# 64-key attention blocks in two-tile and eight-tile shapes, V projected by tokens, in a two-layer transformer kernel

## The chip, the cores and the metric

The kernel runs on one core of a Trainium2 chip. The metric is device time in microseconds (us) from one launch; lower is better. The engines of the core run side by side and each works through its own list in order: TensorE (PE; PEld is its weight load), VectorE (DVE), ScalarE (ACT), GpSimd (POOL) and SyncE (SP), which issues nearly all DMAs.

## The reference

Twice over, a residual attention and a residual token mixer, on S = 2048 tokens of D = 512 features in bf16 (F = 1792; shortened here):

```
def _A_ref(x, wqkv, wo):
    H = 32; Dh = D // H; W = 256
    qkv = (x @ wqkv).reshape(B, S, 3, H, Dh)
    scores = jnp.einsum("bhqd,bhkd->bhqk", q, k) * (Dh ** -0.5)
    mask = (idx[:, None] - idx[None, :] >= 0) & (idx[:, None] - idx[None, :] < W)
    p = _softmax(jnp.where(mask, scores, -1e9), axis=-1)
    return jnp.einsum("bhqk,bhkd->bqhd", p, v).reshape(B, S, D) @ wo
def _B_ref(x, w1, b1, w2, b2):
    u = _gelu(jnp.einsum("bsd,sf->bdf", _layernorm(x), w1) + b1)
    return (jnp.einsum("bdf,fs->bds", u, w2) + b2).transpose(0, 2, 1)
x = x + _A_ref(_layernorm(x), A_wqkv, A_wo)
x = x + _B_ref(_layernorm(x), B_w1, B_b1, B_w2, B_b2)
x = x + _A_ref(_layernorm(x), A_wqkv, A_wo)
x = x + _B_ref(_layernorm(x), B_w1, B_b1, B_w2, B_b2)
```

## The kernel before

Everything stays in on-chip memory between the stages. Weights and x come by DMA on SyncE's queue; only the result goes back.

**Attention.** A layer is cut into four quarters Q of 512 queries and, in each, four groups t of eight heads. A 128-row block of q or k holds the eight heads of a group, 16 rows each. For a group the keys come in blocks of 32, in nine steps m (`NB = 9`: 256 keys of window and one block); in step m each 32-query block i meets the key block kb = i - (i - m) % 9, so that one step fills 512 query columns with up to three runs of columns (`bank_segments`). The scores use the array as four tiles of 64x64 (line 797): r picks the upper or lower 64 rows, c the even or odd heads; k_sb holds each 32-key block twice, with one head of a pair zeroed in each copy, and q_sb holds q twice, even and odd 32-row strips.

```
for r in range(2):
    rows = slice(64 * r, 64 * r + 64)
    for c in range(2):
        last = e.matmul(ps[64 * c:64 * c + 64, 2 * half + r, 32 * i0:32 * i1],
                        lhsT=k_sb[rows, ring, t, kb % 16, :], rhs=q_sb[rows, t, c, 32 * i0:32 * i1],
                        start=True, stop=True, skip_group_check=True, tile_position=(64 * r, 64 * c))
```

The result of a step fills two PSUM banks (0 and 1, or 2 and 3). ScalarE takes the exponential of both into one of six slots of p_sb (line 808, `NSLOT = 6`). VectorE or GpSimd multiplies the 64 columns at the two edges of the window by a triangle (line 825). Then the V product adds the step into banks 4 and 5, again as four 64x64 tiles (line 846); v_all holds V per 32 keys and two heads, with a column of ones for the sum of the softmax. After the ninth step two copies (line 442) take the banks to oU and o2; after each second group, DMAs collect the denominators (den_c) and merge o2 into oU. A quarter later line 871 inverts the denominators, line 889 spreads the inverses over the rows by a matmul, and line 896 multiplies, giving oT, which the output projection (line 762) turns into an addition to x (line 766).

**Side jobs.** Between the steps, TensorE does the work of the next groups: transposes of the normalised x (lines 569 and 582), the projections of K and Q (line 593: four matmuls of the full 128x128 array, 512 columns each), and of V (line 697, also the full array, weights stationary, so that V comes out with its features on the rows). V is then turned by a 32x32 transpose on VectorE (line 700) and spread with zeros into v_all (line 712, VectorE, GpSimd or ScalarE). Line 634 masks K on its way to k_sb; four small DMAs carry q's strips from qt to q_sb. They all use banks 6 and 7.

**The mixer.** The first product (line 987) runs the full array over 16 token tiles for each of 14 blocks of F, then gelu (line 994). For ten of the 14 blocks the lower eight token tiles are done ahead, during the attention, by `paired` (line 609), which works in 64x64 tiles; line 992 adds that part. The second product (line 1033, full array) goes tile by tile into x; in the first layer, its last eight tiles run through `paired` during the second layer's attention.

**The order.** Each engine's list is written out by hand: tables in the file (`LINES`, `ORDER`, `BANKS`), packed as text, say which operation stands where, and the waits between engines follow from what each operation reads and writes. TensorE's matmuls are marked "full" (the 128x128 array) or "cells" (64x64 tiles).

Of the kernel before, what the change touches and what calls it, by code (L numbers as in the profile page):

```python
# [23 lines left out]


# [4 lines left out]
def _table(*text):  # L30
# [5 lines left out]
    'c-pO%NfLlC2n6Z*|D!$VA(pZwQ02iO5IRgWGvj$=s}a1_t)7LW%>DZDUfy1PqA2I%kl8c?b5B|cGg6XlcP%#(x1TjeVa`gOe{yPcK<L$?wAm@}'  # L36
    'VkysiU77XM`Cn79HbaE`*=AYKIH|352Ds;6D^<qc%}i^DBpz)O@D)yLnj()z{$97jIlPxA?E)0O0EP')
ORDER = _table(
    'c-jTQ17HvU00h8C*0OEeT()i7ww7(%wr$(CZSxKgh_DC-BLspY6ao+$$q^f25FX(W5)ly<5fB5B5g(Bd577||DG(D$5C;hn7YPsz8ITC6kqn8E'
    '6xp#48IclckPoSl4QY`HMUW1eksDc%9t{u$Igu4PPyl6+7rBrJg^?eDD2O^JijpXV;;4dRD31~-h0<t`%BYC4D2FDfh6<>ON~nr%sE*pGfm*1C'  # L40
    'uIPhCXo~unfVyaohG>jd7>O2WgJx)nb{K?CXpOe$fR5;lE|`lR=!Ny@hwd1Np6H8F7=XbThHVH!e+<QNOha#sz!)6D5RAuYjKeI9#bivyOiaWi'
    'Ou=-_!3@mCJj};gEW`pV#R)9OA}ql&ti&p;zz3|w2JFTfY{EKh#8xcE4s5}8?7~hw#%0{a9_+_Ktj1m(z-HXT5gf)boWe((!BL#YN!-9C9LH&#'
    '!$n*Lc?B164cGAlw{R1;aR+hu0Qd0-uka90@dPjM9Ix>b&+rzB_y+Is4quR*pYR=@@eO|vnqL9_#xI!v@E2kThGZIsWf(?aAWJYZgE2fKF)G6`'
    'fH7Esu^5HX8J9m1it!nfu^EpE8Jr22go&Ay$(WJRn35@&nyHwU*_e(Q7?GKoo|%}HjhKZwn4P(pn|V2ytyq)!nUjT>hxu5LMOc)DS%Ae^ip5xl'
    'l~|r7S(T+(ku_L_)mWC5S&Ow<opo8C^;m}u*?>*ioNd^WP1u3W*qWW$j&0eVo!F5**o{5ei(T1;ec7A+*^gs6h{M>J137|2IGm$6n%y~plNiLI'
    'oXU|L&xstv>72r8oW<E3$C;eRxm>{cT*yUS#-&`z6<ovRoWnlc#?{=-bzIMD+`!3P!d+a<jl9gOyuwx7#GAa%&Ai1M+`{eL!L8iMJ>1Lv+{cqV'
    '!Bf1z(>%^&yvU<G$0Iz$!#u!)Jj+8o&-=W@+q}a^e9Gs1$9sIhXMD&f{K&g}%ny9cmwdw)e8snX&)@vaPyE7f45LW;&Y%2B3;Mx7{L7U3MJc!v'
    '=pRFh3awxYp->8^hzhF+3a`wHtf-2q=n7C2MN@1QR9wYUd^J)WB~c=kR&~WwLZwk+C07d7Rc@tMDrHn!^-)%3S4(A3E@e?R<y2nfQGVr90Zmp1'
    '1*)*Rsf-G#go>+_%Bj36sfvOWL)BDKHC0(vRYSE@TlLjYO_Wac)LadeT8-6AEtE;EltanXRPEG8om5h-)m3d(K^@gaWz|!iRZRU<RK3+h1Jz4|'
    ')mOtbK!Y??b<|!XHA15_R!cQn<FsEhH9_MwMUym7(==7nHACGsOS3gs{k2eYG+&FgM9XwktF%%pv|KwiTx+yi>oi6iwN@LnS?je;o3vFsG*R2N'  # L50
    'OIx%@yR}ybbWlfhSjTlpr*uN6bxy~0QfG8t7j;3G^iEH;NY`~)w{=6ebWL}3RrmBn4|P`dO+D8GJ<=Op(FfhvK0Vemeb!sO)_eWXC;ie_z0`O8'
    '(@%ZTU(tVbS1<HR!3@hG9MT^Z%Ap<H-}GDI9N;((ba+R0SVwaNM{-0*bxg;0DJODVM{#_|a6;#B7{_uF$8!QFcVZ`VN~dyCr*L$qab;(87N>So'
    'cXd{0a4u(dI%ju!_jev=b0ODuPUm(}7jy|1aWQ9d8K-qg=XC{_c6nEHK38%z7jR+Ma9P)NRTp;^S9cvZa6>nC6PI&KH+O5davQgEdv|ax_iz{2'
    'bA5MmH#c%m_jNP(a$65}9}jepTX=*Ad6<WKxJP@G$9s%BySFF0pT~KEC%L<)d9tT_fM<E8XLzpXc)pkWh>v-J7kagidaB2Ih}ZbAr+ATPdx=l@'
    'lo$J?k9&oedYM;xmDhT`*Lj0?dY5;5kN0|;cX+G!d!sk`kT-j~xA=hf`Jm7EhR^$wullra`i^h;uJ8G*&-sEc`nF&Aim&;)pZl`!`;i~}i68ix'
    'pZcL+`KA8@K7;B`')
# [255 lines left out]
NB = 9  # L312
# [851 lines left out]
```

## Time and profile before

| | |
|---|---|
| median of 3 runs | 496.06 us (495.64 to 497.09) |
| span of the profiled execution | 495.9 us (the page gives no other time for it) |
| TensorE matmuls | 472.4 us busy, 95% |
| VectorE | 325.5 us, 66% |
| ScalarE | 320.6 us, 65% |
| GpSimd | 211.4 us, 43% |
| granted TensorE clock | 1.00 |

Busy times are averages over stages with different limits. The attentions lie between the first and last exponential of each layer, 15.7 to 162.8 us and 235.8 to 399.6 us. A matmul's duration contains the latency of the pipeline, so several can overlap; the time from one start to the next says more. The first matmul after a change of tile shape is sometimes missing from the records.

### The profile page before, as it was taken

What the parts mean: (1) busy time and instruction counts of PE and PEld (TensorE: products, weight loads), DVE (VectorE), ACT (ScalarE), POOL (GpSimd) and SP (SyncE); (2) the same over time, 40 slices, a digit from 0 to 9 for tenths busy, and PEclk for the clock granted to TensorE, in tenths of its full rate; (3) what the DMA queues carried; (4) which work ended last, traced back from release to release, by engine and by line L of the source; (5) the groups of instructions that cost most, each with busy time, mean ns of one, the idle gap of its engine ahead of it and who ended that gap; (6) DMA issues with size and microseconds to landing.
All of it is one profiled execution on the core that took longest, in us unless ns stands there. A gap on an engine that the chain in (4) does not pass through costs nothing.

```text
span 495.9 us, 19594 instructions
## 1 busy us (share of the span) xinstructions
PE 472.4 (95%) x8478; PEld 272.3 (55%) x8550; DVE 325.5 (66%) x661; ACT 320.6 (65%) x392; POOL 211.4 (43%) x372
## 2 busy tenths in 40 slices
PE   8899999999989999999999998998999999999997
PEld 3455566554767444445555875666557654444444
DVE  7999888977763763357895467976996557331222
ACT  3899999998989403502977779889899941340000
POOL 5889546564664310002676445467475411100000
PEclk9999999999999999999999999999999999999999
DMA  6732212131413631331101321024233464040651
GB/s 211 76 99 82 73 55 82 62 99 43 122 56 114 196 106 58 91 98 52 33 18 42 112 79 48 5 75 140 80 91 109 136 189 130 10 138 33 203 169 63
DMA packets 78597, 45.58 MB, mean 92 GB/s; under 512 B 9008, under 2 KB 77488, under 8 KB 78512
## 3 DMA queue, kind: packets, MB, share of 16 engines
q1 hardware_dynamic: 74640, 44.32, 30.4%
q0 software_dynamic: 3872, 0.02, 1.3%
q8 instruction: 67, 1.10, 0.9%
q14 instruction: 18, 0.15, 0.1%
HBM read 33.56 MB, written 2.10 MB: 72 GB/s over the span
## 4 chain that ended last, share of the span: by engine, by line
PE 78%; DVE 9%; ACT 5%; issue 4%; DMA 2%; SPq 2%; POOL 1%; DVEq 0%; ACTq 0%; POOLq 0%
PE ps L1033 14%; PE ps L987 13%; PE ps L609 12%; PE ps L797 10%; PE ps L846 9%; PE ps L593 7%; PE ps L762 5%; ACT p_sb L808 4%; PE ps L697 4%; PE ps L521 2%; SPq L436 2%; PE ps L889 1%; DMA oU<-o 1%; DVE p_sb L825 1%; DVE vt L700 1%
## 5 line engine op out<-in xcount | busy, mean ns | idle before, releaser
L808 ACT ACTIVATE p_sb<-ps 128x1024 bf16<-128x1024 f32 (+8 forms) x288 | 261.4, 975 | 28.7 <-PE ps L797 24.8
L825 POOL TENSOR_TENSOR p_sb<-p_sb,edge 128x256 bf16<-128x256 bf16 (+2 forms) x266 | 131.2, 499 | 111.7 <-ACT p_sb L808 97.8
L797 PE MATMUL ps<-q_sb,k_sb 64*64 64x288 bf16 (+8 forms) x2816 | 107.9, 249 | 4.5 <-ACT p_sb L808 4.3
L846 PE MATMUL ps<-p_sb,v_all 64*34 64x288 bf16 (+17 forms) x2816 | 89.1, 245 | 1.8 <-DVE p_sb L825 0.8
L797 PEld LDWEIGHTS ps<-q_sb,k_sb 64*64 64x64 bf16 x2816 | 59.1, 106 | 51.4 <-ACT p_sb L808 23.7
L846 PEld LDWEIGHTS ps<-p_sb,v_all 64*34 64x34 bf16 (+1 forms) x2816 | 60.6, 100 | 12.1 <-issue 3.6
L593 PE MATMUL ps<-xhT,wqkv 128*128 128x512 bf16 x212 | 55.3, 380 | 4.1 <-issue 3.0
L539 POOL TENSOR_TENSOR rstd<-vare,mhalf 128x4 f32<-128x4 f32 (+1 forms) x17 | 16.6, 976 | 81.0 <-DVE vare L537 57.3
L825 DVE TENSOR_TENSOR p_sb<-p_sb,edge 128x128 bf16<-128x128 bf16 (+2 forms) x134 | 35.5, 279 | 20.3 <-ACT p_sb L808 18.0
L1037 DVE SCALAR_TENSOR_TENSOR x_sb<-ps,b2col,x_sb 128x512 bf16<-128x512 f32 x23 | 17.0, 748 | 43.3 <-PE ps L1033 42.7
L527 DVE BATCH_NORM_STATS2 stats<-x_sb 128x6 f32<-128x512 bf16 x64 | 42.7, 681 | 0.6
L609 PE MATMUL ps<-xh_sb,w1low 64*64 64x512 bf16 x640 | 41.7, 377 | 0.1
L634 DVE TENSOR_TENSOR k_sb<-ps,half 128x1024 bf16<-128x1024 f32 (+1 forms) x31 | 36.5, 1176 | 5.5 <-PE ps L593 5.0
L549 ACT ACTIVATE xh_sb<-x_sb,shift,rstd 128x512 bf16<-128x512 bf16 x12 | 9.5, 812 | 45.2 <-POOL shift L543 29.4
L1033 PE MATMUL ps<-ubuf,w1buf 128*128 128x512 bf16 x165 | 37.2, 379 | 0.2
L712 POOL TENSOR_TENSOR v_all<-vt,even 128x1024 bf16<-128x1024 f32 (+2 forms) x22 | 33.0, 1504 | 5.0 <-DVE vt L700 2.7
L1033 PE MATMUL ps<-ubuf,oU 128*128 128x512 bf16 x149 | 34.3, 379 | 0.3
L994 ACT ACTIVATE ubuf<-ps,b1col 128x512 bf16<-128x512 f32 x28 | 18.5, 686 | 23.9 <-DVE ps L992 20.0
L697 PE MATMUL ps<-xhT,wqkv 128*128 128x512 bf16 x112 | 30.0, 380 | 3.7 <-issue 1.3
L593 PEld LDWEIGHTS ps<-xhT,wqkv 128*128 128x128 bf16 x240 | 19.4, 98 | 24.8 <-issue 4.2
L992 DVE TENSOR_TENSOR ps<-ps,ubuf 128x512 f32<-128x512 f32 x20 | 14.0, 699 | 26.5 <-PE ps L987 26.4
L762 PE MATMUL ps<-wo_sb,oT 128*128 128x512 bf16 x117 | 29.4, 380 | 1.7 <-issue 0.8
(93 smaller groups left out, 545.5 us busy)
## 6 DMA issues: line engine op xcount, KB each, us to landing
w1buf<-in_B_w_dram SPq DMA_DIRECT2D x30, 256.0 KB
w1buf<-in_B_w_dram SPq DMA_DIRECT2D x42, 128.0 KB
w1low<-in_B_w_dram SPq DMA_DIRECT2D x40, 128.0 KB
oU<-in_B_w_dram SPq DMA_DIRECT2D x18, 256.0 KB
oU<-o SPq DMA_DIRECT2D x16, 256.0 KB
q_sb<-qt SPq DMA_DIRECT2D x120, 32.0 KB
xhT<-in_B_w_dram SPq DMA_DIRECT2D x4, 512.0 KB
k_sb<-in_B_w_dram SPq DMA_DIRECT2D x4, 512.0 KB
```

Source lines behind the costliest of these rows:

```text
L527: dve(lambda e: e.bn_stats(stats[:, t, :], x_sb[:, t, :]), 690, prio, reads=[R("x", t)], writes=[R("stats", t)])
L593: last = e.matmul(ps[:, b, :], lhsT=wqkv[:, c, c0:c0 + P], rhs=xhT[:, buf, c, :], start=(c == 0), stop=(c == 3))
L609: last = e.matmul(ps[64 * h:64 * h + 64, banks[r ^ swap], :], lhsT=lhs(r ^ swap, c, rows, 64 * h), rhs=rhs(r ^ swap, c, rows), start=(c == ...
L634: return e.tensor_tensor(dst, src.unsqueeze(2).to_broadcast([P, n, 2, w]), mask[:].unsqueeze(1).unsqueeze(3).to_broadcast([P, n, 2, w]), o ...
L697: last = e.matmul(ps[:, b, :], lhsT=wv[:, c], rhs=xhT[:, buf, c, :], start=(c == 0), stop=(c == 3))
L762: last = e.matmul(ps[:, b, :], lhsT=oT[:, buf, t, i * P:(i + 1) * P], rhs=wo_sb[:, t, :], start=(t == 0), stop=(t == 3))
L797: last = e.matmul(ps[64 * c:64 * c + 64, 2 * half + r, 32 * i0:32 * i1], lhsT=k_sb[rows, ring, t, kb % 16, :], rhs=q_sb[rows, t, c, 32 * i ...
L808: exps[plan.job] = last_exp[0] = plan.op({ACT: (170 + int(2 * (512 - c0) * 0.84), lambda e: e.activation(p_sb[:, slot, :, c0:512], ps[:, 2 ...
L825: return e.tensor_tensor(v, v, g, op=ALU.mult)
L846: last = e.matmul(ps[64 * r:64 * r + w, B_O + (c ^ r), 32 * i0:32 * i1], lhsT=v_all[rows, pos - 32 * c:pos - 32 * c + w], rhs=p_sb[rows, s ...
L987: r = e.matmul(ps[:, b, :], lhsT=blk[:, sc - 8 * part, (ft % 2) * P:(ft % 2 + 1) * P], rhs=xh_sb[:, sc, :], start=(sc == 8 * part), stop=( ...
L1033: r = e.matmul(ps[:, b, :], lhsT=blk[:, turn[n], (st % 2) * P:(st % 2 + 1) * P], rhs=u_at(turn[n]), start=(n == 0), stop=(n == NFT - 1))
```

## The change

Keys come in blocks of 64, in five steps m (`NB = 5`: 256 keys and one block of 64), and each step is made twice, j = 0 and 1, for the even and the odd strips of q. The tiles of all attention work change shape:

- Scores: two tiles of 64x128 instead of four of 64x64. One tile's 128 outputs are 64 keys for two heads, so a step covers four of the group's heads. Two PSUM banks per step, as before; 13 slots of p_sb instead of six.
- V product: one operation takes both halves j of a step, in eight tiles of 64x32. v_all holds V once per 64 keys and head, 16 columns and one of ones.
- V projection: the transposed x is stationary, 64 tokens at a time, and the weights stream (two tiles of 128x64), so V comes out with its tokens on the rows; one copy per 128 tokens puts it into v_all. The transposes on VectorE and the spreading are gone.
- K and Q of a group are projected together by `paired`, which now works in two 64x128 tiles: the two row halves of the array write to two banks and swap banks half-way. The output projection goes through it too, two token tiles at a time, and so does the partial first product of the mixer. The transposes and the spreading of the inverses use 64x128 tiles as well.
- Masks cover the 128 columns at the window's edges.
- Banks 4 to 7 are handed out to V products and side jobs alike, by a table. The order of every engine is new; part of the mixer's partial product starts earlier in the first attention. Four DMAs instead of one merge o2 into oU, two instead of four collect the denominators of two groups.

Cut to its core, the diff is this:

```diff
-NB = 9
+NB = 5
+NSLOT = 13
...
         def emit_scores
...
                     for r in range(2):
-                        rows = slice(64 * r, 64 * r + 64)
-                        for c in range(2):
-                            last = e.matmul(ps[64 * c:64 * c + 64, 2 * half + r, 32 * i0:32 * i1],
-                                            lhsT=k_sb[rows, ring, t, kb % 16, :], rhs=q_sb[rows, t, c, 32 * i0:32 * i1],
-                                            start=True, stop=True, skip_group_check=True, tile_position=(64 * r, 64 * c))
+                        last = e.matmul(ps[:, 2 * h + r, 64 * i0:64 * i1], lhsT=k_sb[tiles_of(r), ring, t, kb % 8, :],
+                                        rhs=q_sb[tiles_of(r), t, j, 64 * i0:64 * i1], start=True, stop=True, skip_group_check=True,
+                                        tile_position=(64 * r, 0))
...
         def emit_pv
...
-                    for c in range(2):
-                        rows = slice(64 * c, 64 * c + 64)
-                        for r in range(2):
-                            pos = v_pos(16 * Q + kb, 2 * t + r)
-                            w = 64 if c else VW
-                            last = e.matmul(ps[64 * r:64 * r + w, B_O + (c ^ r), 32 * i0:32 * i1], lhsT=v_all[rows, pos - 32 * c:pos - 32 * c + w],
-                                            rhs=p_sb[rows, slot, r, 32 * i0:32 * i1], start=(m == 0 and n == 0),
...
+                    for j in range(2):
+                        for r in range(2):
+                            for c in range(2):
+                                q = 2 * r + j
+                                at = v_pos(8 * Q + kb, 4 * t + q)
+                                at, w = (at - 15, 32) if c else (at + 1, VW)
+                                last = e.matmul(ps[32 * q:32 * q + w, u.banks[c], 64 * i0:64 * i1], lhsT=v_all[tiles_of(c), at:at + w],
+                                                rhs=p_sb[tiles_of(c), slots[j], r, 64 * i0:64 * i1], start=(m == 0 and n == 0),
+                                                stop=(m == NB - 1 and n == len(segs) - 1), skip_group_check=True,
+                                                tile_position=(64 * c, 32 * q))
...
         def job_v
...
-                for c in range(4):
-                    last = e.matmul(ps[:, b, :], lhsT=wv[:, c], rhs=xhT[:, buf, c, :], start=(c == 0), stop=(c == 3))
...
-            turned = dve(lambda e: e.transpose(vt[:, k, :], ps[:, b, :]), 705, prio, shares=[BK(b)], writes=[R("vt", k)])
...
-                    return e.tensor_tensor(dst, src.unsqueeze(2).to_broadcast([P, n, 2, DH]),
-                                           even[:].unsqueeze(1).unsqueeze(3).to_broadcast([P, n, 2, DH]), op=ALU.mult)
...
+            for k in range(2):
+                def f(e, k=k):
+                    for c in range(4):
+                        for h in range(2):
+                            last = e.matmul(ps[tiles_of(h), b, 256 * k:256 * k + 256], lhsT=xhT[:, buf, c, i * P + 64 * k:i * P + 64 * k + 64],
+                                            rhs=wqkv[:, c, 2 * D + 256 * h:2 * D + 256 * h + 256], start=(c == 0 and k == 0),
+                                            stop=(c == 3 and k == 1), skip_group_check=True, tile_position=(0, 64 * h))
...
+            copy_out(dst, ps[:, b, :].rearrange("p (k a d) -> p k a d", k=2, a=16), u, 0, 512, [R("v", kb // 2)], tag="Vc")
...
         def paired
...
                             for r in range(2):
-                                rows = slice(64 * r, 64 * r + 64)
-                                for h in range(2):
-                                    last = e.matmul(ps[64 * h:64 * h + 64, banks[r ^ swap], :], lhsT=lhs(r ^ swap, c, rows, 64 * h),
...
+                                last = e.matmul(ps[:, u.banks[r ^ swap], :], lhsT=lhs(r ^ swap, c, tiles_of(r)), rhs=rhs(r ^ swap, c, tiles_of(r)),
+                                                start=(c == chunks[0] and swap == 0), stop=(c == chunks[-1] and swap == 1),
+                                                skip_group_check=True, tile_position=(64 * r, 0))
...
+        def job_kq(Q, t):
+            ring, buf = Q % 2, Q % 2
+            u = paired(range(4), 2, lambda j, c, rows: wqkv[rows, c, (1 - j) * D + t * P:(1 - j) * D + (t + 1) * P], lambda j, c, rows: xhT[rows, buf, c, :],
+                       lambda cs: [R("wqkv", 0), R("wqkv", 1)] + turned(buf), "KQ")
...
         def job_outproj
+            u = paired((0, 2, 1, 3), 2, lambda j, c, rows: oT[rows, buf, c, (i + j) * P:(i + j + 1) * P], lambda j, c, rows: wo_sb[rows, c, :],
+                       lambda cs: [R("wo", n) for n in range(2)] + [R("oT", buf, c) for c in cs], "O")
...
```

1189 lines of the change are left out of this document (536 added, 653 removed).

## The prediction

> **What bounds the kernel now.** I read the stages first. The stretches are cut at the first and last exponential of each quarter (512 queries) of the two attentions: A0 to A3, the tail of layer A, B0 to B3, the tail of layer B.
>
> ```profile
> core 0: us, PE busy (x) PEld busy (x) DVE busy (x) ACT busy (x) POOL busy (x), PEclk, DMA share, GB/s
> 15.70:49.10 33.40, 31.36 (x579) 17.22 (x580) 32.28 (x81) 31.25 (x44) 29.19 (x59) 1.00 0.50 95
> 49.10:87.30 38.20, 35.37 (x913) 22.14 (x923) 33.18 (x64) 36.31 (x43) 22.03 (x34) 1.00 0.24 69
> 87.30:125.70 38.40, 35.78 (x874) 20.91 (x886) 30.43 (x60) 35.91 (x41) 22.47 (x35) 1.00 0.23 68
> 125.70:162.80 37.10, 35.33 (x1100) 25.78 (x1095) 20.09 (x35) 35.23 (x39) 20.89 (x39) 1.00 0.34 97
> 162.80:235.80 73.00, 72.29 (x500) 33.69 (x505) 42.13 (x87) 18.62 (x29) 8.40 (x14) 1.00 0.35 101
> 235.80:272.20 36.40, 34.71 (x614) 19.28 (x617) 28.94 (x55) 30.11 (x42) 24.48 (x49) 1.00 0.11 32
> 272.20:318.60 46.40, 44.93 (x1195) 31.81 (x1192) 31.23 (x66) 38.50 (x42) 21.47 (x38) 1.00 0.22 65
> 318.60:361.20 42.60, 40.48 (x1019) 26.03 (x1014) 33.10 (x69) 37.37 (x43) 26.48 (x43) 1.00 0.31 90
> 361.20:399.60 38.40, 37.48 (x1095) 25.74 (x1101) 25.35 (x45) 36.46 (x42) 20.80 (x34) 1.00 0.39 110
> 399.60:495.90 96.30, 92.37 (x572) 43.66 (x574) 37.34 (x66) 14.44 (x22) 4.85 (x8) 1.00 0.40 118
> ```
>
> A0 is VectorE's (32.28 of 33.40); A1 to A3 are ScalarE's (36.31 of 38.20) with TensorE just behind; B0 to B2 and both tails are TensorE's; in B3 the two are level. The DMA engines are busy half the time at most. So a saving on TensorE is worth its full size in B and the tails, and in A little unless ScalarE gets less too.
>
> Next the groups of instructions (count | busy us, mean ns of one).
>
> ```profile
> L808 ACT ACTIVATE p_sb<-ps 128x1024 bf16<-128x1024 f32 (+8 forms) x288 | 261.4, 975 | 28.7 <-PE ps L797 24.8
> L797 PE MATMUL ps<-q_sb,k_sb 64*64 64x288 bf16 (+8 forms) x2816 | 107.9, 249 | 4.5 <-ACT p_sb L808 4.3
> L846 PE MATMUL ps<-p_sb,v_all 64*34 64x288 bf16 (+17 forms) x2816 | 89.1, 245 | 1.8 <-DVE p_sb L825 0.8
> L700 DVE STREAM_TRANSPOSE vt<-ps 128x512 f32<-128x512 f32 x32 | 22.7, 711 | 6.1 <-PE ps L697 6.1
> ```
>
> TensorE's and ScalarE's means contain pipeline latency, so I take their prices from starts: the chain that ended last, then timelines of ScalarE and TensorE.
>
> ```profile
> 469.99 9.06 PE ps L1033 x42
> ```
> ```profile
> 139.01 3.77 ACT L808 ACTIVATE p_sb<-ps 128x1024 bf16<-128x1024 f32 x4
> ...
> 160.93 0.61 ACT L444 ACTIVATE ubuf<-ps 128x512 f32<-128x512 f32 x1
> 161.40 1.04 ACT L808 ACTIVATE p_sb<-ps 128x1024 bf16<-128x1024 f32 x1
> ```
> ```profile
> 88.24 0.61 PE L846 MATMUL ps<-p_sb,v_all 64*34 64x224 bf16 x16
> 88.68 0.39 PE L797 MATMUL ps<-q_sb,k_sb 64*64 64x64 bf16 x12
> 89.00 1.04 PE L697 MATMUL ps<-xhT,wqkv 128*128 128x512 bf16 x4
> 89.97 0.24 PE L797 MATMUL ps<-q_sb,k_sb 64*64 64x96 bf16 x4
> ```
> ```profile
> 376.92 0.64 PE L889 MATMUL ps<-rc,spread 64*64 64x128 bf16 x32
> 377.39 0.85 PE L846 MATMUL ps<-p_sb,v_all 64*34 64x32 bf16 x36
> ```
>
> A unit of 512 columns takes 9.06/42 = 0.2155 us. Two V-product steps of 512 columns last 0.44, so four 64x64 tiles do run at once. Scores to a full-array projection: 0.32 where 0.22 is work; projection to scores: 0.97 where 4 x 0.2155 is work. So one change of tile shape costs 0.095 to 0.10. An exponential takes (3.77 - 1.03)/3 = 0.91, a 512-column copy on ScalarE 0.48. The dense stretch has 32 matmuls and 32 weight loads in 0.47 us, 7.3 ns each.
>
> **The change, part by part.** Instruction counts and engines come from the order tables of the diff.
>
> *Scores and V product.* Before: 288 steps, 270 units of columns for scores and 270 for the product (the first quarter is shorter). After: 320 score steps of half the heads and twice the keys, 300 units; 160 product steps with eight tiles at once, 150 units. TensorE: 30 x 0.2155 = +6.5 and -120 x 0.2155 = -25.9. No row shows 64x128 or 64x32 tiles. For the scores two tiles write as many partitions per column as the four do now, so I take 0.2155. The product still has 2816 matmuls, on half the columns: 35 instructions in 0.20 us, 5.7 ns each, against the 7.3 seen. Ends: 32.3 us in all (eight at once), 5632 x 7.3 ns = 41.1, 64.6 (four at once, as now). I take 32.3, the row of tiles that run side by side being nearest, and keep both others.
>
> *Exponentials.* 288 to 320, which hurts ScalarE: a full quarter goes from 36 x 0.91 = 32.8 to 36.4. The first quarter, by the row of each width less the 0.12 of overlap, goes from 25.3 to 28.0. Its other work in attention falls: in A from 20 operations to 13 copies of 0.48.
>
> *Masks.* 400 to 480 operations on twice the elements. VectorE has 134 of 35.5 us now; then 87 x 0.253 + 99 x 0.347 + 56 of a 128x512 form that no row shows, 0.35 (its half) to 0.70, taken at 0.535 by the slope between the 128x128 and 128x256 rows: 86. GpSimd goes from 131 to 157, with room (A1: 22 of 38).
>
> *V token-wise.* On TensorE the same 128 units in 128x64 tiles. Gone: 32 transposes (22.7) and the spreading by line 712 (19.7 on VectorE, 33.0 on GpSimd). Added: 32 copies of 0.68. VectorE, all in: A0 34.2, A1 30.6, A2 34.3, A3 29.4, B 20.4, 38.3, 32.9, 29.8 (row durations, less 0.08 each, by which neighbours overlap).
>
> *Side jobs in 64x128 pairs.* The same units, but transposes 32 to 18 (-3.0). Each pair waits once for its own first half before the banks swap; in the new order a score step stands in all but a few of these places, so I cost it at nothing; left bare, such a hole is 0.24 us in the trace, and 49 more of them 12 us at worst. Behind the waiting half, the next scores stand in TensorE's queue, and ScalarE waits for those.
>
> *Changes of shape.* 200 before (100 into the full array, 100 out). After: 236, of which 150 between scores and V product, which were one shape, 72 around the V projection, 14 around the full array. At 0.095: +3.4. No row has a change that leaves 64 rows as they are; ends 0 (a drain gives nothing back) and 0.3; I take 0.095, the one change that the trace prices.
>
> The Trainium skill, "TensorEngine Tiling (Array Packing)", section Tiling Modes, says that changing the tiling mode, not just the tile, drains the TensorE; it speaks against this change, and here the trace agrees at 95 ns. By it all 236 count (484); were only changes of the full array to cost, the sum would be some 10 us lower (474).
>
> *DMA.* The merge of o2 into oU becomes 64 transfers instead of 16, the denominators 32 instead of 64, SyncE's list 398 instead of 377; at a DMA share of 0.5 or less, and ahead of a normalisation that comes 4 us into the next quarter, I cost it at nothing; uncovered it shows as VectorE waiting for oU (now 2.6 us), twice that at worst.
>
> *Order.* More of the partial W1 product and the output projection lies inside the attention: 12 steps of line 609 and 7 projections stand behind B3 now, 2 and 4 equivalents then, which alone takes 32 units, 6.9 us, off the tail of B and puts them where ScalarE sets the pace.
>
> **The sum**, stage by stage. Columns: time before; TensorE's sum before and after (units and changes of shape); ScalarE and VectorE after; forecast.
>
> ```
>         before  PE  ->  PE    ACT   DVE   forecast
> start    15.7                              15.7
> A0       33.4  30.2   27.8   29.4  34.2    35.0
> A1       38.2  35.0   31.7   36.9  30.6    38.0
> A2       38.4  34.2   34.3   38.9  34.3    40.0
> A3       37.1  32.6   34.6   37.9  29.4    39.0
> A tail   73.0  72.4   68.6                 69.2
> B0       36.4  34.2   33.0   31.0  20.4    34.6
> B1       46.4  43.4   37.5   38.2  38.3    40.2
> B2       42.6  39.1   42.3   40.1  32.9    44.4
> B3       38.4  35.3   34.0   37.4  29.8    38.5
> B tail   96.3  92.9   85.9                 89.3
> sum     495.9                             483.9
> ```
>
> Now the stages take 1.03 to 1.09 times their busiest engine. The new pieces of side work are half as long (0.43 for 0.87), so a score waits less: I take 1.03 where ScalarE or VectorE leads and 1.05 where TensorE does; tails keep their present surplus (0.6 and 3.4). The span lies 0.16 under the median of the runs (495.9, 496.06): 484.
>
> **Rivals.**
>
> Smooth: every stage at its busiest engine, no waits: 473. For it: 13 slots of p_sb instead of 6. Against: no quarter does so now. 0.17.
>
> As ragged as now (1.055 and 1.07): 490, still faster, within the forecast's spread; with half of the swaps bare as well, 496, no change that can be measured (within about 0.3%). 0.08 for no change.
>
> Slower, by the V product: eight 64x32 tiles do not run at once. At four, 71 units more per attention, 15.3 us: in A, TensorE rises to 143.7, level with ScalarE's 143, some 157 in place of 152; in B 162 x 1.06 = 172 in place of 158; tails +1.7: 505. It decides from the point where a step costs over 0.35 us. The 7.3 ns per instruction alone gives 488. 0.14.
>
> The Trainium skill, "TensorE: Matmul & The Clock Gate", has a floor of about 25 ns from one matmul's start to the next; on 2816 matmuls an estimate of 70 us, near the four-at-once end. The trace disagrees across tiles: 14.7 ns in the dense stretch.
>
> Slower, by the changes of shape: the 120 in A have 15 us of TensorE's slack behind ScalarE; the 115 outside have none. Each 0.1 more costs 11.5 outside, so at 0.2 a change the gain is gone; at 0.3 it is 23 + 9 more, 516. For it: the shapes are new. Against: 95 ns in both directions now. 0.11.
>
> **The numbers.** The forecast with its spread (478 to 491) has 0.50. Faster: 0.50 + 0.17 = 0.67; same 0.08; slower 0.14 + 0.11 = 0.25. The range runs from the smooth case to the slow V product, 473 to 505, and leaves out the dear changes of shape and a little below.
>
> **What would show it.** Right: the product's step near 0.21 us for both halves together; 0.1 us at each change between score and product; ScalarE over 95% busy in A1 to A3 and A about 5 us longer; B about 6 shorter; tails about 4 and 7 shorter. Wrong: A shorter than 147 (ScalarE was not the bound), or TensorE idle in B with ScalarE not busy, which would be order or masks.

## The result, and the profile after

The changed kernel takes **525.21 us** (median of 4 runs, 522.84 to 525.63) beside 496.01 us for the kernel before on the same chip: a ratio of 1.0577, 95% interval 1.0550 to 1.0604. It is 29 us slower; the prediction said 12 us faster. Its profiled execution spans 523.9 us. Of the experiments further down, one run each of e2 (519.34 us) and e9 (508.13) was over 1.5% above the fastest of its kernel and is left out of the medians.

First the stages, cut as in the prediction at the first and last exponential of each quarter (stretch, its length, then busy time of each engine with its number of instructions, granted clock, DMA share, GB/s).

```profile
core 0: us, PE busy (x) PEld busy (x) DVE busy (x) ACT busy (x) POOL busy (x), PEclk, DMA share, GB/s
...
13.60:50.40 36.80, 31.17 (x578) 15.71 (x574) 33.79 (x87) 31.70 (x44) 26.30 (x48) 1.00 0.33 89
50.40:95.20 44.80, 38.08 (x754) 19.58 (x750) 38.39 (x78) 38.51 (x41) 28.27 (x41) 0.92 0.19 45
95.20:138.60 43.40, 38.34 (x848) 19.89 (x842) 34.64 (x72) 40.61 (x45) 26.96 (x39) 1.00 0.33 40
138.60:185.20 46.60, 39.98 (x816) 21.52 (x817) 32.57 (x68) 39.63 (x44) 20.78 (x35) 0.96 0.41 104
185.20:257.00 71.80, 69.13 (x513) 32.06 (x522) 33.35 (x67) 18.58 (x31) 4.99 (x7) 1.00 0.34 87
257.00:292.80 35.80, 34.88 (x596) 18.16 (x592) 24.20 (x55) 33.29 (x46) 21.34 (x41) 1.00 0.25 66
292.80:339.00 46.20, 40.96 (x912) 22.73 (x909) 40.01 (x96) 39.47 (x45) 23.75 (x32) 1.00 0.29 73
339.00:389.40 50.40, 44.77 (x856) 23.41 (x830) 38.54 (x83) 41.55 (x48) 29.84 (x39) 1.00 0.24 60
389.40:432.40 43.00, 37.77 (x808) 19.70 (x804) 32.95 (x72) 38.50 (x43) 19.17 (x28) 1.00 0.41 103
432.40:523.90 91.50, 85.55 (x517) 39.89 (x526) 31.26 (x57) 12.21 (x20) 2.42 (x4) 1.00 0.43 122
```

Against the rows of before: A takes 171.6 us instead of 147.1, A's tail 71.8 instead of 73.0, B 175.4 instead of 163.8, B's tail 91.5 instead of 96.3. Both tails lie within 3 us of the forecast (69.2 and 89.3), though they became shorter by 1 and 5 us where 4 and 7 were forecast. The whole loss lies in the attentions, and there most stages have no full engine: in A1 the busiest has 38.51 of 44.80 us (ScalarE, 86%), with VectorE's 38.39 beside it; A3 has 86% (TensorE), B1 to B3 89 to 90%. Before, the busiest engine filled 93 to 98% of each quarter.

The granted clock of TensorE also fell, as the page shows it in 40 slices of the span (tenths of full speed):

```profile
PEclk9999799999989999999999999999999999999999
```

In the trace it is 0.50 from 59.0 to 65.8 us (in A1) and from 154.5 to 157.9 us (in A3), and 1.00 elsewhere. TensorE is busy almost throughout these 10.2 us at half speed, which takes about 5 us of its time; the kernel before has none of this inside its span but the last 0.4 us.

The groups of instructions (count | busy us, mean ns | idle before, and what ended it):

```profile
L632 ACT ACTIVATE p_sb<-ps 128x1024 bf16<-128x1024 f32 (+4 forms) x320 | 288.4, 980 | 40.4 <-PE ps L623 28.0
L648 POOL TENSOR_TENSOR p_sb<-p_sb,edge 128x256 bf16<-128x256 bf16 (+2 forms) x238 | 153.8, 666 | 131.7 <-ACT p_sb L632 109.6
L623 PE MATMUL ps<-q_sb,k_sb 64*128 64x320 bf16 (+4 forms) x1408 | 118.5, 258 | 14.2 <-ACT p_sb L632 6.0
L648 DVE TENSOR_TENSOR p_sb<-p_sb,edge 128x256 bf16<-128x256 bf16 (+2 forms) x242 | 89.0, 398 | 19.9 <-ACT p_sb L632 15.8
...
L666 PE MATMUL ps<-p_sb,v_all 64*32 64x320 bf16 (+9 forms) x2816 | 50.7, 260 | 12.8 <-DVE p_sb L648 6.6
```

Busy times are near the forecast: 89.0 us of masks on VectorE (86 forecast), 153.8 on GpSimd (157), exponentials at the price of before. The V product's 2816 matmuls are the same number as before on half the columns, 50.7 us for 89.1. What has grown is the idle time: 12.8 us before the product (L666), about half of it for VectorE's masks, where it was 1.8, and 40.4 before the exponentials, where it was 28.7. TensorE's timeline at the start of A2 gives the new prices:

```profile
95.68 0.41 PE L666 MATMUL ps<-p_sb,v_all 64*17 64x320 bf16 x16
96.02 0.40 PE L623 MATMUL ps<-q_sb,k_sb 64*128 64x64 bf16 x6
96.35 0.41 PE L666 MATMUL ps<-p_sb,v_all 64*17 64x64 bf16 x24
96.70 0.39 PE L623 MATMUL ps<-q_sb,k_sb 64*128 64x192 bf16 x4
```

A score step (L623) and a product step (L666, both halves of a step at once) start 0.33 to 0.35 us apart where 0.2155 is work: eight 64x32 tiles do run at once, and a change of shape costs 0.11 to 0.13.

Last the chain that ended last, by engine: before, then after.

```profile
PE 78%; DVE 9%; ACT 5%; issue 4%; DMA 2%; SPq 2%; POOL 1%; DVEq 0%; ACTq 0%; POOLq 0%
```

```profile
PE 47%; DVE 27%; DMA 9%; ACT 6%; issue 5%; SPq 4%; POOL 2%; DVEq 0%; POOLq 0%; ACTq 0%
```

Where TensorE had 78% of the chain, it now has 47%; VectorE rose from 9 to 27, DMA and SyncE's queue (SPq) together from 4 to 13. More of the chain runs through other engines while TensorE waits. One such place, in B2, from the chain in order of time (start, us, what):

```profile
345.40 0.59 SPq L357
...
346.03 3.81 DMA oU<-o
...
349.92 0.70 DVE oT L714
...
350.67 0.62 PE ps L707 x16
351.29 1.73 PE ps L515 x16
353.01 0.22 PE ps L623 x4
```

and VectorE's and TensorE's timelines beside it (in brackets the idle time before, and what ended it):

```profile
347.69 0.80 DVE L648 TENSOR_TENSOR p_sb<-p_sb,edge 128x256 bf16<-128x256 bf16 x1
349.92 0.69 DVE L714 TENSOR_TENSOR oT<-oU,ps 128x512 bf16<-128x512 f32 x1 [1.44 <-DMA oU<-o]
```

```profile
348.17 0.61 PE L515 MATMUL ps<-ubuf,w1buf 64*128 64x512 bf16 x4
350.67 0.62 PE L707 MATMUL ps<-rc,spread 64*128 64x128 bf16 x16 [1.88 <-DVE oT L714]
351.12 1.89 PE L515 MATMUL ps<-ubuf,w1buf 64*128 64x512 bf16 x16
352.85 0.38 PE L623 MATMUL ps<-q_sb,k_sb 64*128 64x192 bf16 x4
```

SyncE's queue passes one transfer each 0.6 us, and a merge of o2 into oU stands in it behind a strip of q. Its issue starts at 345.40, and the transfer lands 3.81 us after 346.03. VectorE's normalisation (L714) waits 1.44 us for it, the next spreading (L707) waits for a bank that the normalisation reads, so TensorE stands still for 1.88 us, and behind that in TensorE's list are the next pieces of side work and the next scores.

### The profile page after: what moved, and what is told of

It reads as the page before. It is cut to its first block, busy times and chain, and to the rows that moved or that the text cites. A ratio compares the mean times of both kernels' runs of the same rounds, so it can differ in the third digit from the quotient of the medians.

```text
span 523.9 us, 16970 instructions
## 1 busy us (share of the span) xinstructions
PE 472.1 (90%) x7190; PEld 238.3 (45%) x7206; DVE 348.8 (67%) x765; ACT 339.8 (65%) x412; POOL 208.9 (40%) x330
## 4 chain that ended last, share of the span: by engine, by line
PE 47%; DVE 27%; DMA 9%; ACT 6%; issue 5%; SPq 4%; POOL 2%; DVEq 0%; POOLq 0%; ACTq 0%
PE ps L820 13%; PE ps L515 12%; PE ps L795 7%; DVE p_sb L648 7%; PE ps L623 6%; ACT p_sb L632 5%; PE ps L666 5%; DMA oU<-o 4%; DVE stats L444 4%; SPq L357 4%; DVE x_sb L723 3%; PE ps L599 2%; DVE k_sb L544 2%; DVE qt L364 2%; DMA q_sb<-qt 1%
## 5 line engine op out<-in xcount | busy, mean ns | idle before, releaser
L632 ACT ACTIVATE p_sb<-ps 128x1024 bf16<-128x1024 f32 (+4 forms) x320 | 288.4, 980 | 40.4 <-PE ps L623 28.0
L648 POOL TENSOR_TENSOR p_sb<-p_sb,edge 128x256 bf16<-128x256 bf16 (+2 forms) x238 | 153.8, 666 | 131.7 <-ACT p_sb L632 109.6
L623 PE MATMUL ps<-q_sb,k_sb 64*128 64x320 bf16 (+4 forms) x1408 | 118.5, 258 | 14.2 <-ACT p_sb L632 6.0
L648 DVE TENSOR_TENSOR p_sb<-p_sb,edge 128x256 bf16<-128x256 bf16 (+2 forms) x242 | 89.0, 398 | 19.9 <-ACT p_sb L632 15.8
L623 PEld LDWEIGHTS ps<-q_sb,k_sb 64*128 64x128 bf16 x1408 | 52.5, 95 | 87.4 <-ACT p_sb L632 35.4
L515 PE MATMUL ps<-xhT,wqkv 64*128 64x512 bf16 x496 | 68.7, 379 | 3.0 <-issue 1.0
L666 PE MATMUL ps<-p_sb,v_all 64*32 64x320 bf16 (+9 forms) x2816 | 50.7, 260 | 12.8 <-DVE p_sb L648 6.6
L515 PE MATMUL ps<-xh_sb,w1low 64*128 64x512 bf16 x320 | 43.9, 377 | 3.4 <-DMA w1low<-in_B_w_dram 1.1
L666 PEld LDWEIGHTS ps<-p_sb,v_all 64*32 64x32 bf16 (+1 forms) x2816 | 29.5, 89 | 33.3 <-DVE p_sb L648 12.7
L515 PE MATMUL ps<-wo_sb,oT 64*128 64x512 bf16 x256 | 35.8, 389 | 3.3 <-DVE oT L714 2.6
L599 PE MATMUL ps<-wqkv,xhT 128*64 128x256 bf16 x512 | 35.2, 276 | 1.8 <-issue 1.3
L544 DVE TENSOR_TENSOR k_sb<-ps,half 128x1024 bf16<-128x1024 f32 x26 | 31.4, 1209 | 2.4 <-PE ps L515 2.4
```

Of the source, the lines that this page charges most:

```text
L515: last = e.matmul(ps[:, u.banks[r ^ swap], :], lhsT=lhs(r ^ swap, c, tiles_of(r)), rhs=rhs(r ^ swap, c, tiles_of(r)), start=(c == chunks[0 ...
L544: return e.tensor_tensor(dst, src.unsqueeze(2).to_broadcast([P, n, 2, w]), mask[:].unsqueeze(1).unsqueeze(3).to_broadcast([P, n, 2, w]), o ...
L599: last = e.matmul(ps[tiles_of(h), b, 256 * k:256 * k + 256], lhsT=xhT[:, buf, c, i * P + 64 * k:i * P + 64 * k + 64], rhs=wqkv[:, c, 2 * D ...
L623: last = e.matmul(ps[:, 2 * h + r, 64 * i0:64 * i1], lhsT=k_sb[tiles_of(r), ring, t, kb % 8, :], rhs=q_sb[tiles_of(r), t, j, 64 * i0:64 * ...
L632: exps.append(do({ACT: (171 + int(2 * (512 - c0) * 0.832), lambda e: e.activation(p_sb[:, slot, :, c0:512], ps[:, 2 * h:2 * h + 2, c0:512] ...
L648: return e.tensor_tensor(v, v, g, op=ALU.mult)
```

## The experiments

Each time is the median of the runs; the ratio is to the kernel before, on the same chip. The kernel before took 496.0 to 497.5 us beside them. Theories: V, the masks set the pace; S, ScalarE does; D, SyncE's queue does; O, many small waits between lists whose order fits other durations than the chip's.

**One thing cut, in the order given.** e1 to e3 cut the masks to 8 columns, on both engines, on GpSimd alone and on VectorE alone:

```diff
-                def f(e, c=c, ec=ec, w=w, k=k):
+                def f(e, c=c, ec=ec, w=w, k=k, thin=False):
+                    w = 8 if thin else w
...
-                do({DVE: (..., f), POOL: (..., f)}, ...
+                do({DVE: (..., lambda e, f=f: f(e, thin=True)), POOL: (..., lambda e, f=f: f(e, thin=True))}, ...
```

> The changed kernel with every mask operation on both engines cut to 8 columns (most of the masking is left out; number, order and waits of all operations stay). Theory V: the pace of the attention is set by VectorE's in-order list, which carries the masks (89.0 us there) between the copies that free PSUM banks. Then some 50 us of VectorE's work go, about 35 of them in places where TensorE waits behind it: 500 to 508 us. Theory S (ScalarE's exponentials are the bound, as the forecast had it): nothing, 523 to 526. Theory O (waits between queues and the written order, whichever engine's work is lighter): 515 to 525.

> The changed kernel with only GpSimd's mask operations cut to 8 columns (that masking is left out). GpSimd is idle half of the attention, so by its own time nothing is won. Theory V with contention: VectorE's masks are slowed by GpSimd's (128x256: median 0.284, mean 0.378 us); their means fall to 0.22, 0.29 and 0.43, VectorE's masks from 89 to some 70 us, and the time falls to 510 to 517. Without contention: 522 to 526.

> The changed kernel with only VectorE's mask operations cut to 8 columns (that masking is left out). Theory V: nearly all of what the cut on both engines gives, 500 to 510. Theory S or O: 518 to 526.

Measured: e1 513.03 us, ratio 1.0334 (1.0316 to 1.0352); e2 515.53, 1.0360 (1.0308 to 1.0412); e3 515.96, 1.0386 (1.0367 to 1.0404). The masks are worth 12 us, less than theory V asked and a little more than theory O, and either engine's alone give three quarters of it or a little more (e3 lies between what its theories expected). e2 also shows one engine lengthening the other's work: VectorE's masks by shape, in the changed kernel and then in e2, where GpSimd's are thin.

```profile
L648 DVE TENSOR_TENSOR p_sb<-p_sb,edge 128x256 bf16<-128x256 bf16 x99 | 36.1, 381 | 5.4 <-POOL p_sb L648 3.0 <-ACT p_sb L632 1.9 <-issue 0.2
L648 DVE TENSOR_TENSOR p_sb<-p_sb,edge 128x512 bf16<-128x512 bf16 x56 | 31.6, 571 | 7.0 <-ACT p_sb L632 7.0
...
L648 DVE TENSOR_TENSOR p_sb<-p_sb,edge 128x128 bf16<-128x128 bf16 x87 | 25.6, 306 | 7.5 <-ACT p_sb L632 6.9 <-POOL p_sb L648 0.6
```

```profile
L649 DVE TENSOR_TENSOR p_sb<-p_sb,edge 128x256 bf16<-128x256 bf16 x99 | 26.8, 287 | 7.8 <-ACT p_sb L632 3.8 <-POOL p_sb L649 3.3 <-issue 0.2
L649 DVE TENSOR_TENSOR p_sb<-p_sb,edge 128x512 bf16<-128x512 bf16 x56 | 23.4, 426 | 5.0 <-ACT p_sb L632 4.7
...
L649 DVE TENSOR_TENSOR p_sb<-p_sb,edge 128x128 bf16<-128x128 bf16 x87 | 19.6, 239 | 7.5 <-ACT p_sb L632 7.4
```

The same instructions take 0.24, 0.29 and 0.43 us beside thin GpSimd masks and 0.31, 0.38 and 0.57 beside whole ones. The Trainium skill, "SBUF — State Buffer", section SBUF: two separate sides, says that a VectorE operation with two SBUF inputs and a GpSimd operation that reads SBUF lock the same pair of ports for the length of an instruction, and the other blocks; the trace agrees, at 28 to 34% more time for VectorE.

e4 halves the exponentials after the first 60 steps (and inverts a constant instead of den_c):

```diff
+            lo, hi = (c0, 512) if n < 60 else (c0, (c0 + 512) // 2) if n // NSLOT % 2 else ((c0 + 512) // 2, 512)
...
-                p_sb[:, slot, :, c0:512], ps[:, 2 * h:2 * h + 2, c0:512], ACTF.Exp
+                p_sb[:, slot, :, lo:hi], ps[:, 2 * h:2 * h + 2, lo:hi], ACTF.Exp
```

> The changed kernel with the exponentials after the first 60 steps on half of their columns (the other half of p_sb keeps what an earlier step left) and the denominators' inverse taken of a constant. ScalarE's exponentials fall from 288 to about 165 us. Theory S: the attentions shrink towards TensorE's sum, 128 and 147 us, total 470 to 480. Theory V: a small gain from scores whose banks come free sooner, 517 to 523.

Measured: 526.65 us, ratio 1.0594 (1.0553 to 1.0635). ScalarE's busy time falls by 90 us and the kernel doesn't get faster. Theory S, which asked for 470 to 480, is out. Theory V's 517 to 523 isn't met either, but the clock blurs a difference of that size: it averaged 0.98 to 0.99 in the four runs of e4 and 0.990 to 0.997 in those of the changed kernel, which can hide some 3 us.

> The changed kernel with both cuts at once: every mask on 8 columns instead of up to 128 (VectorE and GpSimd), and after the first 60 score steps every exponential on half its columns, the inverse of the denominators taken from a constant. Left out: most of the masking, half of the exponentials, the inverses. Alone the masks gave 12 us, the exponentials nothing. If the two causes simply add, 511 to 515. If the queues are coupled (each waits for whichever neighbour is late, so that one cut alone only moves the wait to the next), the two together give more than their sum: 488 to 503, with TensorE's busy time in the attentions over 93%. If TensorE's own work were the bound, 513 with TensorE hardly idle.

e5, both edits: 506.87 us, ratio 1.0214 (1.0152 to 1.0275). The masks alone gave 12.2, the exponentials -1.4, both 18.3: more than the sum, though by less if the lower clock of e4 hid a part of its gain, and between what the two theories expected.

```diff
             for q in range(4):
...
-                load(oU[rows, buf, t0:t0 + 2, :], o2[rows, :, :], 1 << 16, reads=second, ..., tag="merge")
+                gone = q > 0
+                load(..., reads=[] if gone else second, writes=[] if gone else [...], tag="gone" if gone else "merge")
...
-        line = {e: [self.ops[n] for n in LINES[e]] for e in self.ENGS}
+        line = {e: [self.ops[n] for n in LINES[e] if self.ops[n].tag != "gone"] for e in self.ENGS}
```

> The changed kernel with one merge DMA for each two groups instead of four (the strips of q = 1 to 3 of o2 are left unmerged, so three quarters of that half of the attention output is stale): 48 of SyncE's 398 issues are gone, 28 us of its queue, all inside the attentions. Theory D (the q loads stand behind the merges on SyncE's queue, and scores and normalisation wait for them): 511 to 518, the 8 us of TensorE's waits for q mostly gone. Theory O (many small waits of a tightly written order, of which this is one): 520 to 525.

e6: 512.27 us, ratio 1.0294 (1.0267 to 1.0321): 13 us for 48 DMAs of 64 KB, within the range of theory D. In the chain of e6 DMA and SPq have 4% instead of 13:

```profile
PE 51%; DVE 29%; ACT 9%; issue 4%; DMA 4%; POOL 2%; SPq 0%; DVEq 0%; POOLq 0%; ACTq 0%
```

The path that theory D named isn't the one, though: TensorE's waits for q, which it expected mostly gone, hardly fell (the changed kernel, then e6: waiting engine and line, what for: us, times, longest).

```profile
PEld ps L623 <- DMA q_sb<-qt: 7.2, 8, 2.2
PE ps L623 <- DMA q_sb<-qt: 4.7, 5, 2.0
```

```profile
PEld ps L623 <- DMA q_sb<-qt: 6.0, 6, 1.8
PE ps L623 <- DMA q_sb<-qt: 4.1, 4, 1.5
```

What went is the place shown above: the normalisation's waits for merges fall from 5.8 us to none, and the waits of TensorE's matmuls for the normalisation (oT) from 5.8 to 0.9 us, those of its weight loads from 9.1 to 3.8.

So masks and merges each give 12 to 13 us. Two full causes would explain 25 of the 29 us; the next run shows that they aren't two causes.

**The order.** e8 leaves every operation as it is, on its engine, and replaces the tables:

```diff
-BANKS = _table(...)
-LINES = {"tensor": _table(...), ...}
+BANKS = _table(...)
+LINES = {"tensor": _table(...), ...}
```

Banks 4 to 7 are shared out anew. TensorE's list moves 426 of 1038 operations by at most 18 places, VectorE's 647 of 765, SyncE's 372 of 398, ScalarE's 54 of 400, GpSimd's 238 of 326.

> The changed kernel's operations on the same engines, none left out, in another order of each list and other PSUM homes: the tables were searched anew for the shortest replay with the durations, landings and shape changes that the trace of the changed kernel shows, over four scatterings of them. The replay puts it 19 us under the order given with mean durations, 37 with scattered ones. Theory O (the written order does not fit the durations on the chip): 495 to 508. If the masks, the SyncE queue or the chain through one step's exponential, mask and V product set the time whatever the order: 518 to 526.

Measured: 506.31 us, ratio 1.0182 (1.0143 to 1.0221). Nineteen us come back with nothing left out: two thirds of the loss go away with another order and sharing of banks. The same search was not tried on the kernel before, so what it would win there isn't known. Its stages A1 to A3 and B1 to B3 (columns as above):

```profile
core 0: us, PE busy (x) PEld busy (x) DVE busy (x) ACT busy (x) POOL busy (x), PEclk, DMA share, GB/s
...
48.30:89.20 40.90, 35.49 (x752) 18.97 (x752) 37.31 (x82) 38.32 (x42) 29.36 (x44) 1.00 0.21 49
89.20:132.00 42.80, 37.42 (x858) 19.83 (x864) 37.34 (x75) 40.37 (x46) 27.25 (x39) 1.00 0.36 51
132.00:173.40 41.40, 38.37 (x797) 19.73 (x796) 30.85 (x65) 39.46 (x43) 20.48 (x34) 1.00 0.49 125
...
280.90:323.70 42.80, 41.22 (x904) 22.44 (x910) 38.39 (x93) 39.62 (x45) 24.55 (x34) 1.00 0.30 72
323.70:372.20 48.50, 45.20 (x896) 23.80 (x899) 38.95 (x84) 42.04 (x49) 29.35 (x38) 1.00 0.26 62
372.20:413.20 41.00, 37.73 (x804) 19.18 (x797) 30.84 (x69) 38.92 (x43) 19.34 (x27) 1.00 0.45 115
```

A1 went from 44.8 to 40.9 us with 38.3 us of ScalarE's work as before, now 94% of it; a part of that is the clock, which is 1.00 throughout this execution (in the other three runs of e8 it averages 0.993). Then the cuts once more, in the order of e8:

> The order of e8 with every mask on 8 columns (most of the masking is left out). In the order given this cut gave 12 us, in the order of e8 (506.3) the masks may have found cover. Theory F (a fitted order hides what is off the busiest engines, so the masks' price was the order's): 501 to 506. Theory C (the coupling of exponential, mask and V product stays whatever the order): 12 us again, 492 to 497.

> The order of e8 with half of each exponential after the first 60 steps left out and the inverse taken from a constant. In the order given this gave nothing. In the order of e8, 18 us of TensorE's waits inside the attentions are for exponentials and ScalarE is busy 0.94 of the stages A1 to A3: if ScalarE now sets the pace there, as the forecast had it, 488 to 498; if queues and masks still do, 502 to 507.

> The order of e8 with one merge DMA for two groups instead of four (three quarters of that half of the output is not merged). In the order given this gave 13 us. Theory F (in a fitted order the q loads no longer stand behind the merges): 501 to 506. If SyncE's 28 us are a price by themselves: 492 to 497.

> The order of e8 with the three cuts at once: masks on 8 columns, half of each exponential after the first 60 steps and the inverse from a constant, one merge DMA for two groups instead of four. One by one they gave 4, 2 and 0.5 us there. If what is left is the coupling of these feeds (one stands in for another), together 12 to 20 us: 486 to 494. If it lies elsewhere (TensorE's own list, the copies that free its banks, the K and Q chain), the sum of the three or little more: 497 to 501.

> The order of e8 with masks on 8 columns and half of each exponential left out after the first 60 steps (the inverse from a constant); the four merges stay. All three cuts together gave 485.9, the masks alone 502.1, the exponentials alone 504.6. If the pair that stand in for each other are exponential and mask, the two links of the chain from score to V product: 485 to 491, the merges worth 0 to 4 more. If the merges are one of the pair: 496 to 501.

> The order of e8 with masks on 8 columns and one merge DMA for two groups; the exponentials are whole. If exponential and mask are the pair: 499 to 503, little more than the masks alone. If masks and merges are the pair (both end in VectorE's list): 487 to 494, and the exponentials have room.

| cut | order given | gain | order of e8 | gain | ratio in the order of e8 |
|---|---|---|---|---|---|
| none | 525.2 | | 506.3 | | 1.0182 (1.0143 to 1.0221) |
| masks | 513.0 | 12.2 | 501.2 | 5.1 | 1.0087 (1.0053 to 1.0121) |
| exponentials | 526.7 | -1.4 | 504.6 | 1.7 | 1.0154 (1.0112 to 1.0196) |
| merges | 512.3 | 12.9 | 505.8 | 0.5 | 1.0186 (1.0160 to 1.0211) |
| masks, exponentials | 506.9 | 18.3 | 493.7 | 12.6 | 0.9928 (0.9903 to 0.9953) |
| masks, merges | | | 498.1 | 8.2 | 1.0031 (1.0009 to 1.0053) |
| all three | | | 485.9 | 20.4 | 0.9803 (0.9755 to 0.9852) |

(us; the gains are differences of medians from several sessions, good to some 2 us.) The merges' 13 us vanish in a fitted order: they hung on how the lists were written. So does more than half of the masks' 12. One by one the three cuts now give 7 us, together 20: the feeds stand in for one another, and what one cut frees is mostly taken by a wait for another feed. Masks and exponentials together give nearly twice their parts (12.6 against 6.8); masks and merges give 8.2 against 5.6, which the 2 us hardly tell apart. Both pairs end between what their theories expected, and the third pair, exponentials and merges, was not run. The chain of e12 has TensorE's share of before again:

```profile
PE 78%; DVE 7%; DMA 5%; ACT 4%; SPq 2%; issue 2%; POOL 1%; DVEq 0%; POOLq 0%; ACTq 0%
```

e13 tries the other suspect in that order, the copies out of the banks that a pair of tiles holds:

```diff
         def copy_out(dst, src, use, k, n, writes, engines=(DVE, ACT), small=False, tag="", **kw):
...
+            if copies[tag] > {"Tc": 8, "Qc": 7, "oc": 16, "Vc": 16, "Pc": 10}[tag]:
+                dst, src = half_of(dst), half_of(src)
...
```

> The order of e8 with the copies that empty the side jobs' banks (transposes, K, Q, the output of the V product, the partial first product, and V in the second layer) on half their columns from the third quarter on; half of what they carry is left out. TensorE's waits for a bank that another side job still holds come to some 17 us inside the attentions of e8 (8.7 and 7.7), against 4 to 6 for masks. If a pair that takes two banks at once is what costs: 494 to 499, and most of it in the third and fourth quarter of A and in B. If not: 502 to 506.

500.33 us, ratio 1.0102 (1.0064 to 1.0141): 6 us, between what the two theories expected; B becomes 4.9 us shorter, A hardly. A part of the rest, but this cut also relieves VectorE and ScalarE, so it doesn't tell the banks from the load.

e15 searched again, with operations free to change engine:

> The changed kernel's operations, none left out, in an order searched longer and from another start, with operations free to move between VectorE, ScalarE and GpSimd (166 leave VectorE, most of them masks and copies that trade places). The replay puts it level with e8 (496.0 against 496.9 over scattered durations). If the order is the only thing left, this finds a few us more: 498 to 504. If e8 is already near what this design gives on such lists: 503 to 509.

507.26 us, ratio 1.0228 (1.0193 to 1.0264). Two searches from different settings end within a microsecond; whether an order exists that beats the kernel before stays open, and none of these versions does with all its work in it.

**The masks in the kernel before.** e7 widens them to twice their columns, e14 cuts them to 8:

```diff
-                def f(e, c=c, ec=ec, w=w, k=k):
+                def f(e, c=c, ec=ec + 64, w=w, k=k):
+                    left = min(max(w // 2, c + 288 * (k - 1) + 2 * w - 512), c - c0)
+                    c, ec, w = c - left, ec - left, 2 * w
...
```

```diff
-                def f(e, c=c, ec=ec, w=w, k=k):
+                def f(e, c=c, ec=ec, w=8, k=k):
```

> The kernel before with every mask on twice its columns (ones beside the triangles, so the output stays what it was): the elements per mask of the changed kernel, alone. VectorE gets some 25 us more, GpSimd some 40 or more. If longer masks cost by themselves, the 12 us that thin masks gave back in the changed kernel appear here: 505 to 511. If before's order has the room (V product was written one step or more behind the masks, VectorE 66% busy), 496 to 501; then the masks' price in the changed kernel is a matter of its order.

> The kernel before with every mask on 8 columns (most of the masking is left out). Masks on twice the columns cost it 35 us. If its order already rests on the masks' length, thin ones give 3 to 12: 485 to 493. If it has cover for them as they are and only the doubled ones break it, nothing: 494 to 497.

e7: 532.51 us, ratio 1.0705 (1.0680 to 1.0731), far over what was expected. e14: 495.80, ratio 0.9985 (0.9966 to 1.0003). So in the kernel before the masks cost at most 2 us, and twice as many elements cost 35 us. The waits of e7 (waiting engine and line, what for: us, times, longest) show who pays:

```profile
PE ps L853 <- POOL p_sb L832: 18.2, 39, 1.7
PE ps L853 <- DVE p_sb L832: 4.6, 8, 1.0
```

```profile
L832 POOL TENSOR_TENSOR p_sb<-p_sb,edge 128x512 bf16<-128x512 bf16 (+2 forms) x266 | 210.5, 809 | 69.8 <-ACT p_sb L812 57.6
...
L832 DVE TENSOR_TENSOR p_sb<-p_sb,edge 128x256 bf16<-128x256 bf16 (+2 forms) x134 | 67.9, 522 | 20.7 <-ACT p_sb L812 13.0
```

GpSimd's masks grew from 131.2 to 210.5 us and VectorE's from 35.5 to 67.9, and the V product, 1.8 us of waits before, waits over 20. A cover of that kind has an end, and nothing in the profile of before said where it was: GpSimd was 43% busy.

## Why the prediction was wrong

**Right: the prices.** The V product runs in eight tiles at once: the rival with the slow V product (505) did not happen. TensorE's own work in the attentions, worked out from columns and changes of shape, is some 131 and 149 us, against 128.4 and 146.8 in the sum. The difference is the change of shape: 0.11 to 0.13 us (score and product above) where 0.095 was taken, 4 to 8 us on 236 of them. The rows that the prediction shows give 0.32 - 0.2155 = 0.10 and 0.97 - 0.86 = 0.11, so 0.095 was low for them already. The rival with dear changes (0.2 and more) did not happen either. The Trainium skill, "TensorEngine Tiling (Array Packing)", section Tiling Modes, says that a change of mode drains TensorE; the trace agrees, at that price. Masks, exponentials and copies have the busy times forecast. Of its signs, the product's step came (0.33 to 0.35 us with the change of shape, so about 0.22 without), but not ScalarE over 95% busy in A1 to A3 (86, 94 and 85%), nor A only 5 us longer (24.5), nor B 6 us shorter (11.6 longer).

**Wrong: the stage as its busiest engine times 1.03 to 1.05.** That step turned a nearly right sum into a wrong time. Measured over the busiest engine of the forecast's own columns: A1 44.8/36.9 = 1.21, A2 1.12, A3 1.23, B1 1.21, B2 1.19, B3 1.15. Of the 40.0 us between the forecast's sum and the profiled execution, A has 19.6 and B 17.7. Of these 37, about 5 are TensorE's work and 32 are time that it lost: the forecast left it 23.6 us idle in A and 10.9 in B (stage less its PE column), and the stages less its work leave some 40 and 26. About 5 of these 32 are the half clock in A1 and A3, which the prediction didn't have at all; the other 27 are waits. In e8 some 28 and 21 us are left, in e12 19 and 10, whose 485.9 us is near the 484 forecast; but e12 leaves out half of the exponentials, so it doesn't prove that the forecast could be had. (B1 was also priced at 1.05 although VectorE leads there; by the prediction's own rule it is 39.4, not 40.2.)

The reason given for the small surplus, half as long pieces of side work, was weighed alone. Against it stood what the same sum had found: in A1 to A3, B1 and B2 ScalarE, TensorE and VectorE all at 74 to 97% of the forecast stage, in lists that run in order, with exponential, mask and product in series. e9 to e12, e16 and, more weakly, e5 and e17 show that coupling: the three cuts that give little one by one give nearly three times their sum together, or some twice if the clock of each run is allowed for.

**Wrong: the masks as load alone.** Their size was right to 4%, their place was missing. They lie between the exponential and the product, and the product's halves j now wait for the masks of two steps. Thinning them gives 12 us in the order given and 5 in that of e8.

**Wrong: the merges at nothing.** "Twice that at worst" named the sign in the profile rightly, though not its size: VectorE waits 7.4 us for oU (5.8 in the normalisation, 1.6 in copies) instead of 2.6. And the wait's own length isn't its price. Behind the normalisation TensorE waits for its banks, and taking 48 merges out gave 13 us (e6). The strips of q behind them in SyncE's queue, the other suspect, are waited for almost as long in e6.

**The order** was costed only for the work that it moves, not for whether it fits. The prediction's last line had the sign, "TensorE idle in B with ScalarE not busy, which would be order or masks", yet gave it no price and no rival of its own. e8 puts 19 us on order and banks together.

**The clock** stood nowhere in the prediction. Its price can be estimated from the runs: within the changed kernel and its versions, a run in which the mean clock takes 1 us more from TensorE (the span times what the clock lacks to 1) is on average about 0.7 us longer, an estimate from the clock and span of 80 runs. At 0.990 to 0.997 in the changed kernel that is 1 to 4 of the 29 us. Why the clock fell is not shown.

What stays open: of the 22 us between e8 and the forecast, the coupling of the three feeds accounts for up to 20, but only by runs that leave work out; the copies for some 6 (e13), not told apart from load nor from the 20.

## What to carry to other kernels

Where three engines are each some three quarters busy or more in one stage and feed each other in series, don't price the stage at the busiest one times 1.03: here it was 1.12 to 1.23, and 1.09 to 1.15 after the order was searched anew. Price a wait by what is queued behind it on its engine, not by its own length, and treat cover as finite: here masks that cost 2 us at most under their cover cost 35 when they were doubled. To find such a coupling, cut feeds in pairs as well as one by one.

## What the chip showed that was not expected

A change of tile shape costs about the same for the shapes measured here: from the ends of TensorE's operations in the changed kernel (medians, where no hole lies between), going from 64x128 to 64x32 costs 0.13 us and back 0.11, from 64x128 to 128x64 0.13 and back 0.11. These ends are modelled by the profiler, so the 0.24 us for a change and its way back are better known than the two parts.

The granted TensorE clock fell to 0.50 in two stretches of the changed kernel's attentions, of 6.8 us in A1 and 3.4 in A3. A hole of over 1 us in TensorE lies close by each (1.18 us just before 59.86, 2.14 just before 153.39), but that holes lower the clock is not shown: other holes are not followed by it, and in e8, with less idle time, one execution had none of it and three had a mean clock of 0.993.
